# How a two-phase spectral kernel loads its input: batch-wise loads, contiguous DFT tables, and two frequency tiles at once

## The chip, the cores and the metric

One core of a Trainium2 chip. The metric is the device time of one execution in microseconds (us), as the median of several executions; the profile is one further execution, seen by the hardware profiler. Where a ratio of two kernels is given, it is the mean time of one kernel's fast runs over that of the other's of the same rounds, so it is not quite the ratio of the medians quoted beside it.

Engines: TensorE multiplies matrices and writes PSUM (its accumulator memory), VectorE and ScalarE do element-wise work, GpSimd and SyncE mainly issue DMAs here. In these kernels the loads issued by GpSimd change the type on the way (f32 in memory, f16 in SBUF, the on-chip memory) and appear in the profile as the software queue (q0); the loads issued by SyncE appear as the hardware queue (q1). The profile gives both as shares of the same 16 DMA engines. A packet is one piece of a transfer, as the profile counts it; when a load has landed is the time of landing that the profile gives for it.

## The reference, cut to what matters

```python
# x: [8, 3008, 256] f32, filt_r, filt_i: [1505, 256]
X = np.fft.rfft(x, axis=1)
y = np.fft.irfft(X * (filt_r + 1j * filt_i), n=3008, axis=1)
h = y.reshape(24064, 256) @ w_in           # [256, 2048]
g = h * sigmoid(beta * h)
out = g @ w_out                            # [2048, 256]
```

## The kernel before

Phase 1 is the forward transform, as a product with cosine and sine tables. There are 12 frequency tiles m of 128 rows, 24 row tiles of x (the last with 64 rows, since 3008 = 23 x 128 + 64), and 8 batches of 256 columns. For each m and each half g of the batches, 96 matmuls of 512 columns sum over the row tiles; VectorE multiplies by the filter, and the results go to memory. Phase 2 (inverse transform and the two products with the weights) follows and is not touched.

```python
for g in range(NCOL_GRP):                        # 2 halves of 4 batches
    for t in range(NT):                          # 24 row tiles
        src = x[b0 : b0 + nb, t * P : t * P + L, :].transpose([1, 0, 2])
        nc.gpsimd.dma_start(out=xt[:L, b0 : b0 + nb, :], in_=src)
# ... weights (GpSimd), beta, inverse tables of the first chunk (2 x 1.5 MB), SyncE ...
for src_ap, dst in ((filt_r, flt_r), (filt_i, flt_i)):
    nc.vector.memset(flt_f32, 0.0)
    for t in range(KT):                          # 12 loads; the last has 97 rows
        L = min(P, NF - t * P)
        nc.sync.dma_start(out=flt_f32[:L, t, :], in_=src_ap[t * P : t * P + L, :])
    nc.vector.tensor_scalar_mul(dst, flt_f32, 1.0 / S)
for m in range(KT):                              # 12 frequency tiles
    nc.sync.dma_start(out=tcs,                   # 256 B pieces
        in_=TC_h.rearrange("(t p) k -> p t k", p=P)[:, :, m * P : (m + 1) * P])
    # ... tss the same way ...
    for g in range(NCOL_GRP):
        for nt in range(NT):
            xt, L = x_tiles[nt]                  # L = 64 for the last
            for chk in range(NCH):               # 2 x 512 columns
                nc.tensor.matmul(psA[:, ocol], lhsT=tcs[:L, nt, :], rhs=rhs, ...)
                nc.tensor.matmul(psB[:, ocol], lhsT=tss[:L, nt, :], rhs=rhs, ...)
        # ... six VectorE operations of 128x1024, two stores ...
```

## Time and profile before

| | us |
|---|---|
| median of 4 runs before the prediction | 1852.07 |
| span of the profiled run | 1846.6 |
| first matmul | 52.3 |
| m=0 done (192 matmuls) | 118.8 |
| one group of 96 matmuls from there | 20.93 |
| last matmul of phase 1 starts | 579.1 |

The prediction shows the lines. A line of the page's slices is a picture in time: a column of PE that is not 9 is where something can be won. Here these are the first three, one at the passage to phase 2, and the last; the change is aimed at the first three. And VectorE's first operation after a group is a good timekeeper for TensorE, because the profile names the group's matmuls as what it waited for, and it starts 0.2 us after the start of the last of them (579.27 after 579.08); the distance between two of them is what a group costs. And the cold clock is this in the trace of the kernel before: from 587.3 to 590.7 us, after waits of 5.8 and 1.5 us, eight matmuls start 0.42 us apart instead of 0.216, at a granted clock of 0.50 (1.00 from 592 to 600), which by these starts costs 1.7 us.

### The profile page before, as it was taken

Reading aid. Unit: us, or ns where it says so; the run is one execution under the profiler, and the core shown is the slowest. Engines: PE = TensorE matmul, PEld = TensorE weight load, DVE = VectorE, ACT = ScalarE, POOL = GpSimd, SP = SyncE. Lnnn points to the kernel's source line nnn. Section 1 sums busy time; section 2 is a strip of 40 time slices with the busy share of each in tenths; the row PEclk is TensorE's granted clock in tenths of the full one; section 3 lists DMA queues with packets and bytes.
Section 4 is the critical chain, followed back from the end, with each engine's and each line's share of the span. In section 5 each row is a group of like instructions: output and inputs, shape, how many; then the busy total and the mean of one; then the engine's idle time right before and its main releaser. Section 6 shows DMA issues by size and latency. Waiting matters only on the chain.

```text
span 1846.6 us, 22328 instructions
## 1 busy us (share of the span) xinstructions
PE 1746.4 (95%) x9216; PEld 846.8 (46%) x9216; DVE 796.1 (43%) x1204; ACT 492.0 (27%) x769; POOL 38.9 (2%) x54
## 2 busy tenths in 40 slices
PE   0789999999998999999999999999999999999997
PEld 0234444444443545454455445544545544554553
DVE  1113333333333454444454455545545544544554
ACT  0000000000000433433343343433334434433443
POOL 3310000000000000000000000000000000000000
PEclk9999999999999999999999999999999999999999
DMA  9992222233204545344633644444462464344420
GB/s 213 203 157 58 63 64 58 57 70 78 70 23 155 153 151 177 121 135 152 192 121 111 194 159 140 149 136 160 151 188 86 150 194 138 115 145 150 160 83 22
DMA packets 314682, 235.49 MB, mean 128 GB/s; under 512 B 82962, under 2 KB 308180, under 8 KB 314580
## 3 DMA queue, kind: packets, MB, share of 16 engines
q1 hardware_dynamic: 287412, 219.65, 40.0%
q0 software_dynamic: 27168, 14.42, 5.7%
q8 instruction: 72, 1.18, 0.3%
q14 instruction: 30, 0.25, 0.0%
HBM read 211.23 MB, written 37.22 MB: 135 GB/s over the span
## 4 chain that ended last, share of the span: by engine, by line
PE 82%; DMA 15%; DVE 2%; issue 1%; ACT 0%; POOL 0%; DVEq 0%; SPq 0%; POOLq 0%
PE pso L305 20%; PE psh L286 15%; PE psA L175 13%; PE psB L182 12%; PE psy L255 11%; PE psy L262 11%; DMA out_dram<-osb 8%; DMA xsb<-in_x_dram 6%; DVE osb L316 1%; DMA Qb<-spec_q 0%; DVE gsb L301 0%; ACT sig L294 0%; POOL xsb L122 0%; DVEq L316 0%; SPq L226 0%
## 5 line engine op out<-in xcount | busy, mean ns | idle before, releaser
L294 ACT ACTIVATE sig<-psh,beta_sb 128x512 f32<-128x512 f32 (+1 forms) x768 | 490.8, 675 | 1229.2 <-PE psh L286 1212.6
L301 DVE TENSOR_TENSOR gsb<-psh,sig 128x512 f16<-128x512 f32 (+1 forms) x768 | 492.6, 675 | 511.8 <-ACT sig L294 481.8
L305 PE MATMUL pso<-wq_sb,gsb 128*128 128x256 f16 (+1 forms) x3072 | 492.0, 275 | 18.9 <-DVE osb L316 14.3
L175 PE MATMUL psA<-xsb,tcs 128*128 128x512 f16 (+1 forms) x1152 | 439.2, 383 | 61.1 <-DMA tcs<-dft_tc 52.3
L286 PE MATMUL psh<-yt,w_in_sb 128*128 128x512 f16 (+1 forms) x1536 | 460.2, 375 | 0.0
L182 PE MATMUL psB<-xsb,tss 128*128 128x512 f16 (+1 forms) x1152 | 437.7, 382 | 6.9 <-DMA tss<-dft_ts 6.9
L262 PE MATMUL psy<-uss,Qb 128*128 128x512 f16 (+1 forms) x1128 | 422.4, 374 | 0.0
L255 PE MATMUL psy<-ucs,Pb 128*128 128x512 f16 (+1 forms) x1128 | 422.3, 374 | 0.0
L305 PEld LDWEIGHTS <-gsb 128*128 128x128 f16 (+1 forms) x3072 | 256.8, 98 | 315.5 <-DVE gsb L301 235.6
L175 PEld LDWEIGHTS <-tcs 128*128 128x128 f16 (+1 forms) x1152 | 113.2, 98 | 205.2 <-DMA tcs<-dft_tc 52.3
L182 PEld LDWEIGHTS <-tss 128*128 128x128 f16 (+1 forms) x1152 | 113.1, 98 | 151.1 <-issue 15.9
L286 PEld LDWEIGHTS <-w_in_sb 128*128 128x128 f16 x1536 | 145.2, 98 | 64.6 <-issue 1.7
L262 PEld LDWEIGHTS <-Qb 128*128 128x128 f16 x1152 | 112.8, 98 | 130.3 <-issue 6.9
L196 DVE TENSOR_TENSOR t<-psA,flt_r 128x1024 f32<-128x1024 f32 x24 | 29.4, 1224 | 330.3 <-PE psA L175 330.3
L255 PEld LDWEIGHTS <-Pb 128*128 128x128 f16 x1152 | 112.8, 98 | 126.9 <-issue 6.6
L316 DVE COPY osb<-pso 128x256 f32<-128x256 f32 x192 | 73.8, 419 | 84.1 <-DMA out_dram<-osb 74.2
L270 DVE CAST yt<-psy 128x512 f16<-128x512 f32 (+1 forms) x96 | 64.6, 673 | 43.2 <-PE psy L262 43.2
L122 POOL DMA_DIRECT2D xsb<-in_x_dram x48 | 36.8, 774 | 69.2 <-DMA xsb<-in_x_dram 68.4
L294 ACT ACT_TABLE_LOAD x1 | 1.3, 1283 | 117.8 <-DMA xsb<-in_x_dram 117.8
L199 DVE TENSOR_TENSOR t<-psA,flt_i 128x1024 f32<-128x1024 f32 x24 | 29.4, 1225 | 0.8
L201 DVE TENSOR_TENSOR qst<-t,qst 128x1024 f16<-128x1024 f32 x24 | 29.4, 1224 | 0.8
L198 DVE TENSOR_TENSOR pst<-pst,t 128x1024 f16<-128x1024 f16 x24 | 29.2, 1216 | 0.0
(13 smaller groups left out, 89.7 us busy)
## 6 DMA issues: line engine op xcount, KB each, us to landing
ucs<-dft_uc SPq DMA_DIRECT2D x39, 1536.0 KB, 6.7
uss<-dft_us SPq DMA_DIRECT2D x39, 1536.0 KB, 9.7
out_dram<-osb SPq DMA_DIRECT2D x184, 128.0 KB, 4.5
xsb<-in_x_dram POOLq DMA_DIRECT2D x46, 256.0 KB, 18.3
ucs<-dft_uc SPq DMA_DIRECT2D x8, 1344.0 KB, 6.3
uss<-dft_us SPq DMA_DIRECT2D x8, 1344.0 KB, 8.2
tcs<-dft_tc SPq DMA_DIRECT2D x12, 768.0 KB, 6.7
tss<-dft_ts SPq DMA_DIRECT2D x12, 768.0 KB, 9.6
```

The source lines that it names most:

```text
L122: nc.gpsimd.dma_start(out=xt[:L, b0 : b0 + nb, :], in_=src)
L175: nc.tensor.matmul(psA[:, ocol], lhsT=tcs[:L, nt, :], rhs=rhs, start=(nt == 0), stop=(nt == NT - 1),)
L182: nc.tensor.matmul(psB[:, ocol], lhsT=tss[:L, nt, :], rhs=rhs, start=(nt == 0), stop=(nt == NT - 1),)
L196: nc.vector.tensor_tensor(t1, Av, frb, op=mybir.AluOpType.mult)
L255: nc.tensor.matmul(psy[:, :nl], lhsT=Pb[:, kt, dh * P : (dh + 1) * P], rhs=ucs[:, kt, :nl], start=(kt == 0), stop=False,)
L262: nc.tensor.matmul(psy[:, :nl], lhsT=Qb[:, kt, dh * P : (dh + 1) * P], rhs=uss[:, kt, :nl], start=False, stop=(kt == KT - 1),)
L270: nc.vector.tensor_copy(yt[:, :nl], psy[:, :nl])
L286: nc.tensor.matmul(psh[:, :nl], lhsT=w_in_sb[:, dh, t * P : (t + 1) * P], rhs=yT[dh][:, :nl], start=(dh == 0), stop=(dh == NDH - 1),)
L294: nc.scalar.activation(out=sig[:, :nl], in_=psh[:, :nl], func=mybir.ActivationFunctionType.Sigmoid, scale=beta_sb[:, t : t + 1],)
L301: nc.vector.tensor_mul(gsb[:, :nl], psh[:, :nl], sig[:, :nl])
L305: nc.tensor.matmul(pso[u][:mu, :], lhsT=gsb[:, m0 : m0 + mu], rhs=wq_sb[:, t, :], start=(t == 0), stop=(t == NFT - 1),)
L316: nc.vector.tensor_copy(osb[:mu], pso[u][:mu, :])
```

## The change

Its intent is to feed TensorE earlier. (1) x is loaded batch by batch, in one load of 23 row tiles each; the last 64 rows of all batches come first, into a tile whose other 64 rows are zeros, so that all matmuls have 128 rows. (2) The forward tables are laid out so that each partition reads one piece of 6144 B. (3) The filters are loaded by the software queue, type change included, behind batch 1. (4) beta and the inverse tables move to m=4. (5) A group has two batches, and the groups of m=0 and m=1 are done together, so that each pair of batches feeds both as it arrives.

```diff
+    def col_blocks(T):
+        T = T.reshape(NT, P, KT, P).transpose(2, 1, 0, 3)
+        return np.ascontiguousarray(T.reshape(KT * P, NT * P))
...
-        for g in range(NCOL_GRP):
-            for t in range(NT):
-                src = x[b0 : b0 + nb, t * P : t * P + L, :].transpose([1, 0, 2])
-                nc.gpsimd.dma_start(out=xt[:L, b0 : b0 + nb, :], in_=src)
+        nc.vector.memset(x_sb[LREM:, NTF, :, :], 0.0)
+        nc.gpsimd.dma_start(out=x_sb[:LREM, NTF, :, :], in_=x[:, NTF * P :, :].transpose([1, 0, 2]))
+        for b in range(B):
+            if b == 2:
+                # per filter: memset, one load of 11 tiles, one of 97 rows (both gpsimd), scaling
+            nc.gpsimd.dma_start(out=x_sb[:, :NTF, b, :],
+                in_=x[b, : NTF * P, :].rearrange("(t p) d -> p t d", p=P))
...
-                in_=TC_h.rearrange("(t p) k -> p t k", p=P)[:, :, m * P : (m + 1) * P],
+                in_=TC_h[m * P : (m + 1) * P, :].rearrange("p (t k) -> p t k", k=P),
...
+        for g in range(NG):                      # 4 pairs of batches
+            for j in range(n_pair):              # m = 0 and 1
+                fwd_group(j, g, *pair_cols[j], jtag=str(j))
+        for m in range(n_pair, KT):
+            tcs, tss = load_cols(m)
+            for g in range(NG):
+                stored = fwd_group(m, g, tcs, tss, jtag="0")
+                if m == 4 and g == 0:
+                    with tc.issue_after(...):    # beta and the inverse tables
```

More of the change, by code (lines that the diff above doesn't have):

```diff
@@ L69 @@
     NT = (S + P - 1) // P
+    NTF = S // P
+    LREM = S - NTF * P
     KT = (NF + P - 1) // P
@@ L75 @@
     TCn, TSn, UCn, USn = _dft_tables(S, NF)
+    def col_blocks(T):
+        T = T.reshape(NT, P, KT, P).transpose(2, 1, 0, 3)
+        return np.ascontiguousarray(T.reshape(KT * P, NT * P))
+    TCn, TSn = col_blocks(TCn), col_blocks(TSn)
     TC_h = nc.inline_tensor(TCn, name="dft_tc").ap()
@@ L90 @@
     MMN = 512
-    NCOL_GRP = 2 if (B % 2 == 0 and BD // 2 >= MMN) else 1
-    nb = B // NCOL_GRP
-    GW = nb * D
-    bpc = max(1, min(nb, MMN // D))
-    assert nb % bpc == 0
-    NCH = nb // bpc
+    bpc = max(1, min(B, MMN // D))
+    assert B % bpc == 0
+    NG = B // bpc
+    GWID = bpc * D
     n_chunks = (S + MMN - 1) // MMN
@@ L104 @@
         xsb_pool = ph1.enter_context(tc.tile_pool(name="xsb", bufs=1))
-        col_pool = ph1.enter_context(tc.tile_pool(name="cols", bufs=2))
+        colA_pool = ph1.enter_context(tc.tile_pool(name="colsA", bufs=2))
+        colB_pool = ph1.enter_context(tc.tile_pool(name="colsB", bufs=1))
         flt_pool = ph1.enter_context(tc.tile_pool(name="flt", bufs=1))
@@ L108 @@
         tmpf_pool = ph1.enter_context(tc.tile_pool(name="tmpf", bufs=2))
-        psA_pool = ph1.enter_context(tc.tile_pool(name="psA", bufs=2, space=bass.MemoryType.PSUM))
-        psB_pool = ph1.enter_context(tc.tile_pool(name="psB", bufs=2, space=bass.MemoryType.PSUM))
-        x_tiles = []
-        for t in range(NT):
-            L = min(P, S - t * P)
-            xt = xsb_pool.tile([P, B, D], DT, name=f"xsb{t}")
-            x_tiles.append((xt, L))
-        for g in range(NCOL_GRP):
-            b0 = g * nb
-            for t in range(NT):
-                xt, L = x_tiles[t]
-                src = x[b0 : b0 + nb, t * P : t * P + L, :].transpose([1, 0, 2])
-                nc.gpsimd.dma_start(out=xt[:L, b0 : b0 + nb, :], in_=src)
+        psF_pool = ph1.enter_context(tc.tile_pool(name="psF", bufs=2, space=bass.MemoryType.PSUM))
+        x_sb = xsb_pool.tile([P, NT, B, D], DT, name="x_sb")
+        nc.vector.memset(x_sb[LREM:, NTF, :, :], 0.0)
+        if LREM > 0:
+            nc.gpsimd.dma_start(
+                out=x_sb[:LREM, NTF, :, :],
+                in_=x[:, NTF * P :, :].transpose([1, 0, 2]),
+            )
+        for b in range(B):
+            if b == 2:
+                flt_r = flt_pool.tile([P, KT, D], DT, name="flt_r")
+                flt_i = flt_pool.tile([P, KT, D], DT, name="flt_i")
+                KTF = NF // P
+                for src_ap, dst in ((filt_r, flt_r), (filt_i, flt_i)):
+                    nc.vector.memset(dst, 0.0)
+                    if KTF > 0:
+                        nc.gpsimd.dma_start(
+                            out=dst[:, :KTF, :],
+                            in_=src_ap[: KTF * P, :].rearrange("(t p) d -> p t d", p=P),
+                        )
+                    if NF > KTF * P:
+                        LL = NF - KTF * P
+                        nc.gpsimd.dma_start(out=dst[:LL, KTF, :], in_=src_ap[KTF * P :, :])
+                    nc.vector.tensor_scalar_mul(dst, dst, 1.0 / S)
+            if NTF > 0:
+                nc.gpsimd.dma_start(
+                    out=x_sb[:, :NTF, b, :],
+                    in_=x[b, : NTF * P, :].rearrange("(t p) d -> p t d", p=P),
+                )
         w_in_sb = wsb_pool.tile([P, NDH, DFF], DT, name="w_in_sb")
@@ L128, with load_cols @@
         beta_sb = wsb_pool.tile([P, NFT], F32, name="beta_sb")
-        nc.sync.dma_start(out=beta_sb, in_=moe_beta.rearrange("(t p) -> p t", p=P))
+        def load_cols(m, pool=colA_pool, tag_suffix="0"):
+            tcs = pool.tile([P, NT, P], DT, name=f"tcs{tag_suffix}", tag=f"tcs{tag_suffix}")
+            tss = pool.tile([P, NT, P], DT, name=f"tss{tag_suffix}", tag=f"tss{tag_suffix}")
+            nc.sync.dma_start(
+                out=tcs,
+                in_=TC_h[m * P : (m + 1) * P, :].rearrange("p (t k) -> p t k", k=P),
+            )
+            nc.sync.dma_start(
+                out=tss,
+                in_=TS_h[m * P : (m + 1) * P, :].rearrange("p (t k) -> p t k", k=P),
+            )
+            return tcs, tss
+        pair_cols = (
+            [load_cols(0), load_cols(1, colB_pool, "1")] if KT > 1 else [load_cols(0)]
+        )
         pre_uc = pre_pool.tile([P, KT, MMN], DT, name="pre_uc")
@@ L133 @@
         nl0 = min(MMN, S)
-        nc.sync.dma_start(
-            out=pre_uc[:, :, :nl0],
-            in_=UC_h.rearrange("(t p) n -> p t n", p=P)[:, :, 0:nl0],
-        )
-        nc.sync.dma_start(
-            out=pre_us[:, :, :nl0],
-            in_=US_h.rearrange("(t p) n -> p t n", p=P)[:, :, 0:nl0],
-        )
-        flt_f32 = flt_pool.tile([P, KT, D], F32, name="flt_f32", tag="flt_tmp")
-        flt_r = flt_pool.tile([P, KT, D], DT, name="flt_r")
-        flt_i = flt_pool.tile([P, KT, D], DT, name="flt_i")
@@ L146, with fwd_group @@
-        for src_ap, dst in ((filt_r, flt_r), (filt_i, flt_i)):
-            nc.vector.memset(flt_f32, 0.0)
-            for t in range(KT):
-                L = min(P, NF - t * P)
-                nc.sync.dma_start(out=flt_f32[:L, t, :], in_=src_ap[t * P : t * P + L, :])
-            nc.vector.tensor_scalar_mul(dst, flt_f32, 1.0 / S)
-        for m in range(KT):
-            tcs = col_pool.tile([P, NT, P], DT, name="tcs", tag="tcs")
-            tss = col_pool.tile([P, NT, P], DT, name="tss", tag="tss")
+        def fwd_group(m, g, tcs, tss, jtag):
+            psA = psF_pool.tile([P, MMN], F32, name=f"psA{jtag}", tag=f"psA{jtag}")
+            psB = psF_pool.tile([P, MMN], F32, name=f"psB{jtag}", tag=f"psB{jtag}")
+            b0 = g * bpc
+            for nt in range(NT):
+                L = P
+                rhs = x_sb[:L, nt, b0 : b0 + bpc, :]
+                nc.tensor.matmul(
+                    psA[:, :GWID],
+                    lhsT=tcs[:L, nt, :],
+                    rhs=rhs,
+                    start=(nt == 0),
+                    stop=(nt == NT - 1),
+                )
+                nc.tensor.matmul(
+                    psB[:, :GWID],
+                    lhsT=tss[:L, nt, :],
+                    rhs=rhs,
+                    start=(nt == 0),
+                    stop=(nt == NT - 1),
+                )
+            Av = psA[:, :GWID].rearrange("p (b d) -> p b d", b=bpc)
+            Bv = psB[:, :GWID].rearrange("p (b d) -> p b d", b=bpc)
+            frb = flt_r[:, m, :][:, None, :].to_broadcast([P, bpc, D])
+            fib = flt_i[:, m, :][:, None, :].to_broadcast([P, bpc, D])
+            pst = stg_pool.tile([P, bpc, D], DT, name="pst", tag="pst")
+            qst = stg_pool.tile([P, bpc, D], DT, name="qst", tag="qst")
+            t1 = tmpf_pool.tile([P, bpc, D], F32, name="t1", tag="t1")
+            nc.vector.tensor_tensor(t1, Av, frb, op=mybir.AluOpType.mult)
+            nc.vector.tensor_tensor(pst, Bv, fib, op=mybir.AluOpType.mult)
+            nc.vector.tensor_add(pst, pst, t1)
+            nc.vector.tensor_tensor(t1, Av, fib, op=mybir.AluOpType.mult)
+            nc.vector.tensor_tensor(qst, Bv, frb, op=mybir.AluOpType.mult)
+            nc.vector.tensor_sub(qst, t1, qst)
+            colsl = slice(b0 * D, (b0 + bpc) * D)
@@ L156 @@
             nc.sync.dma_start(
-                out=tcs,
-                in_=TC_h.rearrange("(t p) k -> p t k", p=P)[:, :, m * P : (m + 1) * P],
-            )
-            nc.sync.dma_start(
-                out=tss,
-                in_=TS_h.rearrange("(t p) k -> p t k", p=P)[:, :, m * P : (m + 1) * P],
-            )
-            for g in range(NCOL_GRP):
-                psA = psA_pool.tile([P, GW], F32, name="psA", tag="psA")
-                psB = psB_pool.tile([P, GW], F32, name="psB", tag="psB")
-                b0 = g * nb
-                for nt in range(NT):
-                    xt, L = x_tiles[nt]
-                    for chk in range(NCH):
-                        cb = chk * bpc
-                        rhs = xt[:L, b0 + cb : b0 + cb + bpc, :]
-                        ocol = slice(chk * bpc * D, (chk + 1) * bpc * D)
-                        nc.tensor.matmul(
-                            psA[:, ocol],
-                            lhsT=tcs[:L, nt, :],
-                            rhs=rhs,
-                            start=(nt == 0),
-                            stop=(nt == NT - 1),
-                        )
-                        nc.tensor.matmul(
-                            psB[:, ocol],
-                            lhsT=tss[:L, nt, :],
-                            rhs=rhs,
-                            start=(nt == 0),
-                            stop=(nt == NT - 1),
-                        )
-                Av = psA[:].rearrange("p (b d) -> p b d", b=nb)
-                Bv = psB[:].rearrange("p (b d) -> p b d", b=nb)
-                frb = flt_r[:, m, :][:, None, :].to_broadcast([P, nb, D])
-                fib = flt_i[:, m, :][:, None, :].to_broadcast([P, nb, D])
-                pst = stg_pool.tile([P, nb, D], DT, name="pst", tag="pst")
-                qst = stg_pool.tile([P, nb, D], DT, name="qst", tag="qst")
-                t1 = tmpf_pool.tile([P, nb, D], F32, name="t1", tag="t1")
-                nc.vector.tensor_tensor(t1, Av, frb, op=mybir.AluOpType.mult)
-                nc.vector.tensor_tensor(pst, Bv, fib, op=mybir.AluOpType.mult)
-                nc.vector.tensor_add(pst, pst, t1)
-                nc.vector.tensor_tensor(t1, Av, fib, op=mybir.AluOpType.mult)
-                nc.vector.tensor_tensor(qst, Bv, frb, op=mybir.AluOpType.mult)
-                nc.vector.tensor_sub(qst, t1, qst)
-                colsl = slice(b0 * D, (b0 + nb) * D)
-                nc.sync.dma_start(
-                    out=P_h[m * P : (m + 1) * P, colsl],
-                    in_=pst[:].rearrange("p b d -> p (b d)"),
-                )
-                nc.sync.dma_start(
-                    out=Q_h[m * P : (m + 1) * P, colsl],
-                    in_=qst[:].rearrange("p b d -> p (b d)"),
-                )
@@ new lines, in fwd_group @@
+                out=P_h[m * P : (m + 1) * P, colsl],
+                in_=pst[:].rearrange("p b d -> p (b d)"),
+            )
+            return nc.sync.dma_start(
+                out=Q_h[m * P : (m + 1) * P, colsl],
+                in_=qst[:].rearrange("p b d -> p (b d)"),
+            )
+        n_pair = len(pair_cols)
+        for g in range(NG):
+            for j in range(n_pair):
+                tcs, tss = pair_cols[j]
+                fwd_group(j, g, tcs, tss, jtag=str(j))
+        for m in range(n_pair, KT):
[3 more added lines that the diff above has]
+                if m == 4 and g == 0:
+                    with tc.issue_after(stored.ins if hasattr(stored, "ins") else stored):
+                        nc.sync.dma_start(out=beta_sb, in_=moe_beta.rearrange("(t p) -> p t", p=P))
+                        for pre, U_h in ((pre_uc, UC_h), (pre_us, US_h)):
+                            nc.sync.dma_start(
+                                out=pre[:, :, :nl0],
+                                in_=U_h.rearrange("(t p) n -> p t n", p=P)[:, :, 0:nl0],
+                            )
```

## The prediction

> **What bounds the kernel now.** I read the page's slices and chain first, then TensorE's waits in the opening, then the opening's DMA counts.
>
> The page, busy tenths in 40 slices of 46 us, and the chain:
>
> ```profile
> PE   0789999999998999999999999999999999999997
> ...
> DMA  9992222233204545344633644444462464344420
> PE 82%; DMA 15%; DVE 2%; issue 1%; ACT 0%; POOL 0%; DVEq 0%; SPq 0%; POOLq 0%
> PE pso L305 20%; PE psh L286 15%; PE psA L175 13%; PE psB L182 12%; PE psy L255 11%; PE psy L262 11%; DMA out_dram<-osb 8%; DMA xsb<-in_x_dram 6%; DVE osb L316 1%; DMA Qb<-spec_q 0%; DVE gsb L301 0%; ACT sig L294 0%; POOL xsb L122 0%; DVEq L316 0%; SPq L226 0%
> ```
>
> TensorE bounds everything except the first three slices, where it starves and the DMA engines are full; the 6% of x loads on the chain are those slices. The change touches only phase 1 (forward DFT), so I look at its start. The waits up to 118.8 us:
>
> ```profile
> PE psA L175 <- DMA tcs<-dft_tc: 52.3, 1, 52.3
> ...
> PE psA L175 <- DMA xsb<-in_x_dram: 8.6, 11, 1.3
> ...
> PE psB L182 <- DMA tss<-dft_ts: 6.9, 1, 6.9
> ```
>
> TensorE starts at 52.3 (first cosine columns), stops again until 65.0 (sine columns), then trickles behind x. VectorE's timeline gives the end of each group (a group is 96 matmuls: one frequency tile m, four batches):
>
> ```profile
> 118.82 1.22 DVE L196 TENSOR_TENSOR t<-psA,flt_r 128x1024 f32<-128x1024 f32 x1 [26.80 <-PE psA L175]
> ...
> 139.75 1.22 DVE L196 TENSOR_TENSOR t<-psA,flt_r 128x1024 f32<-128x1024 f32 x1 [13.79 <-PE psA L175]
> ...
> 579.27 1.23 DVE L196 TENSOR_TENSOR t<-psA,flt_r 128x1024 f32<-128x1024 f32 x1 [13.79 <-PE psA L175]
> ```
>
> m=0 is done at 118.8; from there 22 groups take 460.45 us, 20.93 each, with no hole. Two groups of work (41.9 us) took 118.8: the opening loses 77 us, and that is all there is to win in phase 1.
>
> What makes x late? Software-queue packets (x, 512 B written each) in three windows, 10 to 25, 72 to 76 and 95 to 103 us; columns are packets, MB, share of 16 engines:
>
> ```profile
> q0 software_dynamic: 2608, 1.30, 62.5%
> q1 hardware_dynamic: 2609, 2.58, 62.3%
> ...
> q0 software_dynamic: 1516, 0.75, 139.2%
> q1 hardware_dynamic: 63, 0.05, 4.9%
> ...
> q0 software_dynamic: 2153, 1.07, 108.1%
> q1 hardware_dynamic: 156, 0.10, 5.3%
> ```
>
> Nearly alone, x moves 1516/4 = 379 packets per us; in 116 to 119 it is 1111/3 = 370, or 43.2 ns per packet on each of 16 engines. Beside 1 KB hardware packets it gets 174, one for one. In 95 to 103 it gets only 269, although the hardware queue has 20 packets per us. My reading: those are the leftovers of one engine, and a load of x ends when its slowest engine ends. GpSimd's issues in this stretch, each waiting for an older x load, come every 2.15 us (94.47, 96.58, 98.77, 100.91): one load has 512/16 = 32 packets per engine, so the slow engine does 15 per us where 23 are possible. The filter's last rows are 97 partitions, twelve small loads per filter.
>
> [...] the profile does not name engines, so it is an inference. [...] after 8 us idle at 579 us matmuls start 0.43 us apart instead of 0.216. [...] x's last 64 rows are 64-row matmuls, and steps into and out of them are 0.31 us:
>
> ```profile
> 558.15 0.38 PE L182 MATMUL psB<-xsb,tss 64*128 64x512 f16 x1
> 558.46 0.39 PE L175 MATMUL psA<-xsb,tcs 128*128 128x512 f16 x1
> 558.68 0.38 PE L182 MATMUL psB<-xsb,tss 128*128 128x512 f16 x1
> ```
>
> **The change part by part.**
> 1. Matmuls: 12 tiles x 4 groups x 48 = 2304 of 512 columns, as before. The padded tail makes all of them 128-row. Two steps of +0.095 us per 96 matmuls go: a group of 48 costs 48 x 0.216 = 10.36 us instead of 10.47. Over m=2..11 (40 groups) 414.5 us instead of 418.6: 4 us saved on the path, nearly sure.
> 2. Column tables: 6144 B contiguous per partition instead of 24 pieces of 256 B. Four loads (m=0,1), probably six (m=2 has a free buffer): 768 packets, 48 per engine; at the 1 KB packet's 42 ns, 24.4 GB/s, one takes 252 ns: 12.1 us per engine in all, done near 17 us when alternating with x. The 52.3 and 65.0 us waits go.
> 3. The 3 MB of preloaded inverse tables leaves the opening (3072 packets x 42 ns / 16 = 8 us), and lands in m=4, where DMA is at 26%. Filters: twelve hardware loads each become software loads behind batch 1: 3010 packets, 8.1 us of the software queue.
> 4. x by whole batch, groups of two batches, m=0 and 1 together: each arriving pair of batches feeds 96 matmuls, 20.7 us, instead of a trickle for one m.
> 5. VectorE: six operations of 1.22 us become twelve of some 0.65 per 20.7 us: hidden. PSUM still has two buffers per tag.
> 6. The passage to phase 2 (579.3 to 587.3, waiting for Qb) stays: Pb and Qb still take space of the x tiles and wait for the last matmul.
>
> Arrivals, per engine: x tail 32 packets, each batch 184, filters 188. Batches 0,1: 3 (first packet) + 400 x 43.2 ns = 17.3 + 12.1 (tables) + 2 (landing) = 34. Batches 2,3: 956 packets, 41.3, + 12.1 + 1.3 (stores) + 3 + 2 = 60, and up to 64 if each 97-row filter load again sits on one engine (91 extra packets, 4 us). Batches 4,5: 76 to 80. Batches 6,7: 93 to 98.
> TensorE: group 0 from 34, +20.7 +2.3 (cold clock) = 57; group 1 waits for batches 2,3, 60 to 64, then is continuous: + 3 x 20.7 + 0 to 2 (cold again) = 122 to 128. Batches 4 to 7 come in time. Then 414.5: phase 1 ends at 537 to 543 instead of 579.3. Sum: 36 to 43 us, centre 40, so 1852 - 40 = 1812.
>
> **The rivals.**
> A. x stays the bound at its present pace: if the lag is not one engine but the engines' rate with casting (213 packets per us over 24,064 in 113 us), the last batches land near 115, and phase 1 ends at 115 + 20.7 + 414.5 = 550: gain 29, 1823. For: the share is above 90% throughout. Against: 370 in two windows.
> B. The one x tile is tracked as a whole, or by the span of its strided slices, and the first matmul waits for all of x: start 97, end 97 + 83 + 414.5 = 594, 1867. Against: at 579.48 Pb's strided load of batch 0 is issued before the stores of batches 4 to 7 into the same rows at 583.92, so strided pieces are told apart.
> C. The columns of m=2 are issued in order behind the last stores of the pair: TensorE would stall some 10 us after the pair, 1822. Against: the columns of m=1 went out at 68.88 us, before the stores of m=0 at 89.53.
> D. TensorE fills the hole before batches 2,3 with m=2's first group, if the static order allows: no hole at all, phase 1 ends near 34 + 2.3 + 48 x 10.36 = 534: gain 45, 1807. For: the order is not the program's in the kernel before (13 psA, then 13 psB); against: that needs the hole foreseen.
>
> **Range and chances.** 2% is 1815.0, and the sum gives 1809 to 1816 with nothing else going wrong: slightly more than even. A or C in part give 1822 or so, D 1807. Prediction 1812, range 1803 to 1825; faster 0.54, within 2% 0.45, slower 0.01 (B).
>
> **What would show it.** First matmul near 34 us; the wait before group 1 small, 3 to 7 us, and by x; the last batch landed before 100; software packets above 300 per us from 20 us on; no 64-row matmul and 10.36 us from group to group; columns of m=2 landed before 25 us; the Qb wait still about 8 us. I am wrong if group 1 starts after 70, if TensorE waits again after the pair, or if phase 2 (579.3 to the end, 1267 us) changes by more than 3 us.

## The result, and the profile after

The changed kernel takes 1804.52 us (median of 8 runs, 1803.5 to 1806.71) where the kernel before takes 1851.27 (12 runs): ratio 0.975, 95% interval 0.974 to 0.976. That is faster by over 2%, and within the predicted range, near its low end: 46.7 us won where 40 were predicted.

The page's slices and chain after:

```profile
PE   2999999999989999999999999999999999999997
...
DMA  9941321111127356336434643643454354443420
...
PE 85%; DMA 12%; DVE 2%; issue 1%; ACT 0%; DVEq 0%; SPq 0%; POOLq 0%
```

From the second slice on PE is at 9, but for the passage to phase 2 and the last slice. The DMA engines are full for two slices instead of three. TensorE's only wait in the first 125 us, and the two places where it falls (timeline of TensorE; the bracket is the idle time and what ended it):

```profile
PE psA L181 <- DMA x_sb<-in_x_dram: 32.6, 2, 31.7
```

```profile
31.71 0.59 PE L181 MATMUL psA<-x_sb,tcs 128*128 128x512 f16 x1 [31.71 <-DMA x_sb<-in_x_dram]
...
56.22 0.38 PE L181 MATMUL psA<-x_sb,tcs 128*128 128x512 f16 x1 [0.94 <-DMA x_sb<-in_x_dram]
```

The tables no longer appear: TensorE waits for batches 0 and 1 until 31.7, and batches 2 and 3 come 0.94 us late. From there nothing is missing. The ends of groups on VectorE:

```profile
118.36 0.69 DVE L202 TENSOR_TENSOR t<-psA,flt_r 128x512 f32<-128x512 f32 x1 [6.42 <-PE psA L181]
...
128.72 0.69 DVE L202 TENSOR_TENSOR t<-psA,flt_r 128x512 f32<-128x512 f32 x1 [6.42 <-PE psA L181]
...
532.76 0.69 DVE L202 TENSOR_TENSOR t<-psA,flt_r 128x512 f32<-128x512 f32 x1 [6.42 <-PE psA L181]
```

At 118.4 us both m=0 and m=1 are done, where before m=0 alone was done at 118.8: one m more, 2 x 20.93 = 41.9 us of work. After it 40 groups take 414.4 us, 10.36 each, where 40 half groups took 418.6: 4.2 us. Together 46.1, which is the whole shift of the end of phase 1 (last matmul at 532.6 instead of 579.1) but 0.4.

The software queue from 24 to 48 us, while batches and filters pass:

```profile
q0 software_dynamic: 9402, 4.75, 145.5%
```

That is 9402/24 = 392 packets per us, 41 ns per packet and engine, with nothing beside it.

### The profile page after: what moved, and what is told of

Read it like the earlier page. It is cut to its first block, busy times and chain, and to the rows that moved or that the text cites.

```text
span 1804.9 us, 22521 instructions
## 1 busy us (share of the span) xinstructions
PE 1737.0 (96%) x9216; PEld 850.4 (47%) x9216; DVE 809.3 (45%) x1349; ACT 492.8 (27%) x769; POOL 18.4 (1%) x19
## 4 chain that ended last, share of the span: by engine, by line
PE 85%; DMA 12%; DVE 2%; issue 1%; ACT 0%; DVEq 0%; SPq 0%; POOLq 0%
PE pso L330 21%; PE psh L311 16%; PE psA L181 13%; PE psB L188 13%; PE psy L280 11%; PE psy L287 11%; DMA out_dram<-osb 9%; DMA x_sb<-in_x_dram 3%; DVE osb L341 1%; DMA Qb<-spec_q 0%; DVE gsb L326 0%; ACT sig L319 0%; DVEq L341 0%; SPq L251 0%; DVEq L326 0%
## 5 line engine op out<-in xcount | busy, mean ns | idle before, releaser
L181 PE MATMUL psA<-x_sb,tcs 128*128 128x512 f16 x1152 | 438.3, 380 | 32.6 <-DMA x_sb<-in_x_dram 32.6
L188 PE MATMUL psB<-x_sb,tss 128*128 128x512 f16 x1152 | 438.1, 380 | 0.0
L181 PEld LDWEIGHTS <-tcs 128*128 128x128 f16 x1152 | 113.0, 98 | 168.6 <-issue 33.6
L188 PEld LDWEIGHTS <-tss 128*128 128x128 f16 x1152 | 113.0, 98 | 137.9 <-issue 2.9
L202 DVE TENSOR_TENSOR t<-psA,flt_r 128x512 f32<-128x512 f32 x48 | 33.2, 692 | 307.6 <-PE psA L181 307.6
L205 DVE TENSOR_TENSOR t<-psA,flt_i 128x512 f32<-128x512 f32 x48 | 33.2, 691 | 1.7
L207 DVE TENSOR_TENSOR qst<-t,qst 128x512 f16<-128x512 f32 x48 | 33.2, 691 | 1.6
L204 DVE TENSOR_TENSOR pst<-pst,t 128x512 f16<-128x512 f16 x48 | 32.7, 682 | 0.0
L206 DVE TENSOR_TENSOR qst<-psB,flt_r 128x512 f16<-128x512 f32 x48 | 32.7, 681 | 0.0
```

The source lines that it names most:

```text
L181: nc.tensor.matmul(psA[:, :GWID], lhsT=tcs[:L, nt, :], rhs=rhs, start=(nt == 0), stop=(nt == NT - 1),)
L188: nc.tensor.matmul(psB[:, :GWID], lhsT=tss[:L, nt, :], rhs=rhs, start=(nt == 0), stop=(nt == NT - 1),)
L202: nc.vector.tensor_tensor(t1, Av, frb, op=mybir.AluOpType.mult)
L205: nc.vector.tensor_tensor(t1, Av, fib, op=mybir.AluOpType.mult)
```

## The experiments

Eleven runs were made (one of them the changed kernel again), all with correct results. For each I give the median and the ratio to the kernel before of the same rounds, and where the last matmul of phase 1 starts in its trace ("end of phase 1": 579.1 before, 532.6 after). Phase 2 is the same code in all of them.

### One engine's lag (b_split97)

```diff
-                nc.sync.dma_start(out=flt_f32[:L, t, :], in_=src_ap[t * P : t * P + L, :])
+                L16 = L - L % 16
+                nc.sync.dma_start(out=flt_f32[:L16, t, :], in_=src_ap[t * P : t * P + L16, :])
+                if L > L16:
+                    nc.sync.dma_start(out=flt_f32[L16:L, t, :], in_=src_ap[t * P + L16 : t * P + L, :])
```

> The kernel before, with nothing changed but the last filter load of each filter: 97 rows as 96 rows and 1 row[...]. My theory (one engine lags with the 97-row loads and what queues behind them, and every load of x ends with it): x then costs each engine 1504 packets x 41 ns = 62 us, and the hardware packets of that time 31 us (pre-tables 8, filters 8, the tables of m=0 and 1 15), so the last batches land near 98 instead of 117, m=0 ends near 102 instead of 118.8, and the whole is 12 to 18 us faster: 1833 to 1839. Rival A (the engines themselves move casting packets at the pace seen, 213 per us on average): nothing changes, within 2 us of before. Between: 3 to 10 us if the 97 rows are only one of several causes of lag.

Measured: 1840.60 against 1848.46, 7.9 us faster, ratio 0.9957 (0.9943 to 0.9971); end of phase 1 570.9, 8.2 earlier. The direction is that of the theory; the size is not, and lies in the band (3 to 10 us) that I had set for one of several causes. The trace shows the reasons for both. First its windows 68 to 84 and 96 to 104 us:

```profile
q0 software_dynamic: 3886, 1.93, 87.4%
q1 hardware_dynamic: 3885, 0.99, 46.5%
...
q0 software_dynamic: 3155, 1.57, 145.0%
```

When the tables are through, x runs alone at 3155/8 = 394 per us, with no hardware packet left; in the kernel before the prediction saw 269 in the same stretch, with a trickle of 20 hardware packets per us beside it. Nothing but two loads of 97 rows had been split, so a lag of x comes from these loads. That it is one engine that lags is read from the packet lists of the kept traces, which do not name engines: in the kernel before, the 256 B packets between 95 and 103 us start one at a time, 67 ns apart, about the 66 ns that a pair of packets, one of x and one of a table, takes on an engine (below), and from 32 to 38 us the last 1 KB packets of the first filter pass the same way, 95 ns apart; in b_split97 the tables still pass at 244 packets per us from 84 to 88 us, and from 96 us there are none.

Why one engine holds up all of x is in the times of the loads: in the kernel before, from the tenth load on, almost every load of GpSimd is issued 0.3 us after the load eight before it has landed (for example landed at 94.18, next one issued at 94.47). So eight loads, 8 x 32 packets per engine, are in flight, and when one engine is that far behind, the others run out of x: at 109.5 us x falls to 30 packets per us, with 4 hardware packets per us beside it.

The size: while tables pass, the two queues move packet for packet, 3886/16 = 243 pairs per us, so a pair takes 16/243 = 66 ns on an engine, and a 256 B table packet adds 66 - 41 = 25 ns to a packet of x. In the window 10 to 25 us of the kernel before, 174 pairs per us give 92 ns, so a 1 KB packet adds 51. (The single engine's packets, 67 and 95 ns apart, give 26 and 54.) I had reckoned 20 and 42: 20 was an estimate, and 42 is what a 1 KB packet takes nearly alone (in the kernel before 370 of them and 10 of x per us from 5.8 to 6.8 us, 16/380 = 42 ns). With the measured costs I estimate that an engine needs 62 + 380 x 51 ns (inverse tables and filters) + 768 x 25 ns = 100 us for what passes until x is in, not 93. The last load of x landed at 109.4 (117.7 before): the lag was worth 8 us, and most of the rest of the wait was packets.

### The tables alone (b_tab)

The edit is the change's part 2 in the kernel before: `col_blocks` and the two `in_=` lines of the diff above.

> The kernel before, with the forward tables alone laid out so that each partition reads 6144 B in one piece. My theory: the tables of m=0 and 1 are 32 packets per engine instead of 768, which frees 9 us of every engine, and above all leaves the engine with the 97-row loads far fewer packets to alternate with x, so x is throttled much less: the last batches land near 100, first matmul before 45 us, 12 to 20 us faster in all (1831 to 1839). Rival (only the bytes and the first wait count, the lag is elsewhere or is not one engine): the first matmul comes earlier, but m=0 still ends with x near 110 or later: at most 6 to 8 us faster.

Measured: 1837.31, 11.1 us faster, ratio 0.9938 (0.9924 to 0.9952); end of phase 1 567.8. That is 1 us short of my range and above the rival's 6 to 8; but the last load of x landed at 106.4 and m=0 was done at 107.6, nearer to the rival's 110 than to my 100. First matmul at 42.4 as expected, but the lag does not vanish. Its windows 64 to 76 and 88 to 96:

```profile
q0 software_dynamic: 2746, 1.36, 95.5%
q1 hardware_dynamic: 40, 0.08, 2.0%
...
q0 software_dynamic: 3153, 1.57, 144.9%
q1 hardware_dynamic: 7, 0.00, 0.2%
```

From 64 to 76 x gets only 229 per us, and later 394. The 40 hardware packets of the first window again start one at a time, the last at 69.2 us. After it x has the engines to itself and still falls to 26 per us at 70.5 to 71.5 us, about the pace of one engine (1000/41 = 24): the lagging engine is working off its part of the loads in flight. Splitting the 97 rows won 8.2 us of phase 1 and laying out the tables 11.3. Both leave the lagging engine less to do, so they may overlap; no run has both in the kernel before.

### The inverse tables early (a_pre)

In the changed kernel, beta and the inverse tables are loaded ahead of the forward tables:

```diff
+        nc.sync.dma_start(out=beta_sb, in_=moe_beta.rearrange("(t p) -> p t", p=P))
+        for pre, U_h in ((pre_uc, UC_h), (pre_us, US_h)):
+            nc.sync.dma_start(out=pre[:, :, :nl0],
+                in_=U_h.rearrange("(t p) n -> p t n", p=P)[:, :, 0:nl0])
         def load_cols(m, pool=colA_pool, tag_suffix="0"):
...
-                if m == 4 and g == 0:
-                    with tc.issue_after(...):    # the same loads
```

> The changed kernel with the inverse tables for the first chunk (3 MB) and beta loaded at the start, ahead of the forward tables, as in the kernel before. My theory (3072 packets of 1 KB take 8 us of every engine and delay all that comes after): batches 0,1 land near 40 instead of 31.7, batches 2,3 near 64, then TensorE runs without holes: 8 to 9 us slower than the changed kernel, near 1813. Rival (the engines had room[...]): under 3 us.

Measured: 1814.28 against 1848.52, ratio 0.9813 (0.9796 to 0.9829); end of phase 1 544.4, 11.8 later than in the changed kernel. First matmul at 43.1, 11.4 later. The theory holds; most of the size is again that of the 1 KB packet at 51 ns: 192 per engine x 51 = 9.8 us instead of 8. The other 1.6 us were not tested apart; beta, which this edit moves too, goes first as 2048 packets of 4 B and lands at 3.9 us.

### The filters in the hardware queue (a_fltHW)

```diff
-                    nc.vector.memset(dst, 0.0)
-                    nc.gpsimd.dma_start(out=dst[:, :KTF, :], ...)
-                    nc.gpsimd.dma_start(out=dst[:LL, KTF, :], ...)
-                    nc.vector.tensor_scalar_mul(dst, dst, 1.0 / S)
+                    nc.vector.memset(flt_f32, 0.0)
+                    for t in range(KT):
+                        L = min(P, NF - t * P)
+                        nc.sync.dma_start(out=flt_f32[:L, t, :], in_=src_ap[t * P : t * P + L, :])
+                    nc.vector.tensor_scalar_mul(dst, flt_f32, 1.0 / S)
```

> The changed kernel with the filters loaded as in the kernel before: 12 hardware-queue loads each into an f32 tile, the last of 97 rows. If one engine's lag by the 97-row loads were enough by itself, x would be throttled from about 20 us on and batches 2,3 would land 5 to 10 us later, 5 to 10 us slower in all. My theory says that the lag grows only while the lagging engine has many other hardware packets to alternate with (the tables are now 48 packets per engine and land first): batches 2,3 land within 4 us of the changed kernel's 55.6, and the whole is within 5 us of it, 1802 to 1809.

Measured: 1812.60 against 1848.52, ratio 0.9805 (0.9791 to 0.9820); end of phase 1 543.9, 11.3 later. I was wrong: batch 3 landed at 66.4, 10.2 us later than in the changed kernel, and the whole is more than 5 us slower, so the numbers of the other side are the nearer ones. But TensorE does not wait for batches 2 and 3, where I looked. It has one wait, at the start:

```profile
PE psA L177 <- DMA x_sb<-in_x_dram: 45.4, 1, 45.4
```

In the software queue the filters stand behind batch 1. In the hardware queue they stand in no line with x at all: their 1 KB packets pass beside batches 0 and 1 (from 9 to 18 and from 36 to 45 us) and delay them to 45.4. The lag is there too. From 29 to 36 us:

```profile
q0 software_dynamic: 2621, 1.33, 139.9%
q1 hardware_dynamic: 21, 0.11, 4.0%
```

Of the 21 packets 18 are 6144 B pieces of tables (0.11 MB; the others are 4 B). In the packet list they start one at a time, 0.28 us apart, the last at 34.1 us. That is the pace of one engine: in the changed kernel's trace 16 engines, alternating with x from 6 to 14 us, did 55 per us, or 3.4 each. So one engine has a backlog, while x as a whole runs at 2621/7 = 374 per us and not at 269 as in the kernel before. A load of x is now 184 packets per engine instead of 32, so that the loads in flight keep the other engines busy; that this makes the difference was not tested. How much of the 11.3 is the lag and how much the filters' place in front was not separated.

### Without the pair (a_nopair)

```diff
-        pair_cols = (
-            [load_cols(0), load_cols(1, colB_pool, "1")] if KT > 1 else [load_cols(0)]
-        )
+        pair_cols = [load_cols(0)]
```

> The changed kernel without the pairing: m=0 alone first, m=1 after it like the others. My theory (each arriving pair of batches must feed 96 matmuls or TensorE starves): x lands as before, the last pair near 89 us, m=0 ends there + 10.4 = near 100 instead of 118.4 for m=0 and 1 together; the remaining 44 groups x 10.36 us = 456: phase 1 ends near 556 instead of 532.6, 21 to 25 us slower than the changed kernel, 1826 to 1830. Rival (the pairing only reorders work, the gain came from the transfers alone): within 5 us of the changed kernel.

Measured: 1820.96 against 1848.52, ratio 0.9849 (0.9834 to 0.9864); end of phase 1 551.4, 18.8 later than with the pair. Three fifths of the gain survive without the pair, two fifths need it. TensorE's restarts:

```profile
27.97 0.58 PE L179 MATMUL psA<-x_sb,tcs 128*128 128x512 f16 x1 [27.97 <-DMA x_sb<-in_x_dram]
51.52 0.58 PE L179 MATMUL psA<-x_sb,tcs 128*128 128x512 f16 x1 [10.93 <-DMA x_sb<-in_x_dram]
67.94 0.58 PE L179 MATMUL psA<-x_sb,tcs 128*128 128x512 f16 x1 [3.62 <-DMA x_sb<-in_x_dram]
84.01 0.59 PE L179 MATMUL psA<-x_sb,tcs 128*128 128x512 f16 x1 [2.96 <-DMA x_sb<-in_x_dram]
```

From the second on, pairs of batches arrive 16 us apart and feed 10.4 us of work each. After a hole the matmuls are also slower at first: from 51.52 to 56.17 eleven of them start 0.42 us apart, and then 0.22, and the group that began at 67.94 ended at 80.9, 12.9 us instead of 10.4. Of the expected 21 to 25 us, 18.8 came, because x itself is in 5 us earlier (last load landed at 83.9 instead of 89.1): two tables fewer stand before it.

### The 64-row matmuls, from both sides (b_pad, a_tail64)

In the kernel before (b_pad):

```diff
             xt = xsb_pool.tile([P, B, D], DT, name=f"xsb{t}")
+            if L < P:
+                nc.vector.memset(xt[L:, :, :], 0.0)
...
-                        rhs = xt[:L, b0 + cb : b0 + cb + bpc, :]
+                        rhs = xt[:, b0 + cb : b0 + cb + bpc, :]
...
-                            lhsT=tcs[:L, nt, :],
+                            lhsT=tcs[:, nt, :],
```

In the changed kernel (a_tail64):

```diff
-                L = P
+                L = P if nt < NTF else LREM
```

> The kernel before, with the last 64 rows of x padded by zeros to 128 rows in SBUF, so that all matmuls of phase 1 have 128 rows. My theory (each step into and out of the 64-row form costs 0.095 us on TensorE): 22 to 24 groups x 0.19 us = 4.2 to 4.6 us faster, 1846.7 to 1847.1 where before is 1851.3; groups 20.73 us apart instead of 20.93. Rival (the steps hide behind something else, such as the reads at a group's end): no change.

> The changed kernel, with the last tile of x used as 64 rows again (the zero rows are there but not read). My theory (two steps of 0.095 us per group, and the groups are now 48 matmuls): 48 groups x 0.19 us = 9 us slower, 1813.6 where the changed kernel is 1804.5; groups 10.55 us apart instead of 10.36. Rival (the cost goes by the number of 64-row matmuls, which is the same as before): 4.5 us slower. Second rival: no change.

Measured: b_pad 1843.46 against 1848.46, 5.0 us faster, ratio 0.9972 (0.9958 to 0.9986), end of phase 1 574.8 (4.3 earlier), groups 20.72 us apart. a_tail64 1812.08 against the same 1848.46, ratio 0.9801 (0.9788 to 0.9814), where the changed kernel has 0.975; end of phase 1 541.7, 9.1 later. Groups in a_tail64 are 10.57 us apart (108.6, 119.2, 129.7). Its steps:

```profile
107.88 0.38 PE L188 MATMUL psB<-x_sb,tss 128*128 128x512 f16 x1
108.19 0.39 PE L181 MATMUL psA<-x_sb,tcs 64*128 64x512 f16 x1
108.41 0.38 PE L188 MATMUL psB<-x_sb,tss 64*128 64x512 f16 x1
108.72 0.39 PE L181 MATMUL psA<-x_sb,tcs 128*128 128x512 f16 x1
```

Starts are 0.31 us apart at each change of form and 0.22 within one. The number of 64-row matmuls is the same 96 in the kernel before and in a_tail64; the number of changes is doubled, and so is the cost. It goes by the change, not by the matmul.

### The changed kernel again, and m=2's tables later (after_again, a_m2late)

```diff
-                fwd_group(j, g, tcs, tss, jtag=str(j))
+                last = fwd_group(j, g, tcs, tss, jtag=str(j))
+            if g == 1:
+                with tc.issue_after(...last...):
+                    cols2 = load_cols(n_pair)
```

> The changed kernel itself, once more, beside the others of this group: ratio 0.975 to before again (0.973 to 0.977), and its phase 2 as long as that of the kernel before within 2 us, if the 5.5 us by which phase 2 was longer in the first profile of the changed kernel are chance. If they belong to the change, phase 2 is again near 1260 us from its first matmul to its last, against 1255.

> The changed kernel with the columns of m=2 issued behind the last store of the second pair's first two groups, not at the start. My theory (a 6144 B packet costs each engine some 220 ns wherever it stands; 16 packets fewer at the start): first matmul at 28.0 as in the run without pairing, which also had 16 packets fewer, batches 2,3 near 52, the pair done near 114.7 and no wait for m=2's columns: 3 to 4 us faster than the changed kernel. Rival (the early columns ride along for free): the same within 1 us. Rival C of the prediction (late columns stall TensorE after the pair): slower.

Measured: after_again 1804.58 against 1849.95, ratio 0.9755 (0.9742 to 0.9768), phase 1 the same to 0.1 us. Its phase 2, from first matmul to last, is 1258.8 us, after 1260.6 in the first profile and 1255.0 in the kernel before; the other variants of the changed kernel, with the same phase 2, have 1252.2 to 1258.2, those of the kernel before 1254.2 to 1257.1. So neither expectation was met cleanly: there is a scatter of some us from run to run. The medians of all runs say more than single profiles: the whole gain is 46.7 us in the first comparison and 45.4 here, where phase 1 gives 46.5, so that about 1 us at most is left for a longer phase 2. a_m2late: first matmul at 28.0, end of phase 1 528.2, 4.4 earlier; 1802.18, 2.4 faster by the medians, ratio 0.9741 (0.9727 to 0.9754). The trace says that the early tables do not ride for free, and that late ones stall nothing; the intervals of the two ratios overlap, so in the whole time the gain is likely but not shown.

### A version that streams (a_stream, a_stream2)

The wait left is the first 31.7 us. Two batches must be in before anything starts, although one row tile of them is enough for four matmuls.

```diff
+        PIECES = [(0, 6), (6, 12), (12, 18), (18, 23)]   # a_stream2: (0, 2), (2, 6), ...
+        for g in range(NG):
+            for k, (ta, tb) in enumerate(PIECES):
+                for b in range(g * bpc, (g + 1) * bpc):
+                    nc.gpsimd.dma_start(out=x_sb[:, ta:tb, b, :],
+                        in_=x[b, ta * P : tb * P, :].rearrange("(t p) d -> p t d", p=P))
+            # behind g == 1: the filters; the pair's tables in the same pieces
...
+            for nt in range(NT):
+                for j in range(n_pair):                  # m = 0 and 1, tile by tile
+                    # matmul into psA of j, matmul into psB of j
```

> A version that goes further: every pair of batches in four pieces of x's row tiles, the pair's tables in matching pieces, the matmuls of m=0 and 1 taken tile by tile, the filters behind the second pair, the columns of m=2 after the second pair. If TensorE can eat x as it lands (a row tile of two batches is 256 packets, 0.66 us at 389 per us, and feeds four matmuls, 0.86 us), the first matmul comes near 12 us instead of 31.7, the four pairs end near 100 instead of 118.4: 14 to 18 us faster than the changed kernel, 1787 to 1791. If the pieces cost more than they bring (tables of 1.5 KB pieces, cold clock through small holes, filters late for the third pair's PSUM), 5 us or less.

> The streaming version with the first piece of every pair cut down to two row tiles, tables likewise: the first matmul at 9 to 11 us instead of 16.0, so up to 5 us faster than the streaming version (1783.6 beside 1848.5, ratio 0.9653): ratio 0.9625 to 0.9645. If TensorE only starts earlier and then waits for x in many small holes at the cold clock, the ratio stays at 0.965.

Measured: a_stream 1783.60 against 1848.52, ratio 0.9653 (0.9635 to 0.9670), end of phase 1 517.4, 15.1 earlier than the changed kernel, within the 14 to 18 expected. The first matmul is at 16.0, not 12, the fourth pair is done at 103.0, and one of the feared costs came: the filters land at 54.5 us, after the first pair is done (38.6), so VectorE starts late, and at 62.2 us TensorE waits 2.1 us for it to free PSUM. Four edits are in this version; the late tables of m=2 alone gave 4.4 us (a_m2late), and the rest was not separated. The smaller loads cost x no pace: from 24 to 32 us, with loads of 384 KB written, several of them in flight, the software queue moved 3144/8 = 393 packets per us, as with 1472 KB in the changed kernel (392). This version is the fastest kernel together with a_stream2: 1785.02 against 1849.95, ratio 0.9650 (0.9637 to 0.9663), end of phase 1 516.7. The smaller first piece was a miss. TensorE's waits in the first 62 us of a_stream2:

```profile
7.42 0.58 PE L195 MATMUL psA<-x_sb,tcs 128*128 128x512 f16 x1 [7.42 <-DMA x_sb<-in_x_dram]
...
12.96 0.59 PE L195 MATMUL psA<-x_sb,tcs 128*128 128x512 f16 x1 [1.97 <-DMA x_sb<-in_x_dram]
...
23.11 0.58 PE L195 MATMUL psA<-x_sb,tcs 128*128 128x512 f16 x1 [4.92 <-DMA x_sb<-in_x_dram]
```

It starts 8.6 us sooner, and then waits twice more, because x and tables share the engines until 21 us; each restart begins with a matmul of 0.58 us. The rival of the expectation holds.

## Why the prediction was right

By its own steps:

- **What makes x late.** That one engine lags, and by the loads of 97 rows, was a guess from the pace of x; b_split97 bears it out. But the lag is 8 of the 77 us that the opening lost; the larger part was packets in front of x and beside it.
- **Part 1, the padding.** Predicted 4 us, measured 4.2 in the groups, and confirmed from both sides. (So the 77 us of the opening were not "all there is to win in phase 1", as the prediction says before it comes to this part.)
- **Part 2, the tables.** The waits at 52.3 and 65.0 went, m=2's tables went out at the start (issued at 3.3 and 3.8 us), and all had landed by 16.7 us. Predicted near 17. The packet cost was right (6144 B: 16/55 = 291 ns for a packet with its share of x, less 1.09 packets of x at 41, since 481 of x went with 442 of these, = 246; I said 252), but x's first packet came at 5.6, not at 3, so that the first tables had the engines to themselves.
- **Part 3, tables and filters moved.** Right in kind. a_pre and a_fltHW show that each is worth over 11 us in the changed kernel (the tables together with beta); the inverse tables were put at 8. The term that was too small is the 1 KB hardware packet beside x, 51 ns instead of 42. It did not enter the sum, since these loads no longer stand in front.
- **Part 4, the pair.** Right: with it x's arrival (89.1 us) no longer bounds, and TensorE is continuous from 56.2.
- **Parts 5 and 6.** VectorE's operations are 0.69 us and hidden. The passage to phase 2 stays: TensorE waits 5.1 us for Pb and 1.5 more for Qb. Before it was 5.8 and 1.5, but the 5.8 ended with VectorE's last read of psA (585.15); Pb had landed at 584.4. The prediction puts the whole passage down to Qb.
- **The sum.** Batches 0 and 1 came at 31.7 instead of 34, batches 2 and 3 at 56.2 instead of 60 to 64, and the pair was done at 118.4 instead of 122 to 128. This is where nearly all of the 7.5 us between 1812 and 1804.5 lie (0.8 are the kernel before, 1851.3 instead of 1852.1). Two terms were too large: a packet of x takes 41.1 ns alone, not 43.2 (956 x 2.1 ns = 2 us), and the allowance of up to 4 us for 97-row loads on one engine did not come: x ran at 392 per us right through them, and each landed 0.2 us after the filter load before it. The 3 us for the first packet are its time in the kernel before (2.96); the 2 us for landing were an allowance that rested on no trace named there. The slow matmuls at the start cost 2.7 us (13 of them from 31.71 to 37.20, 5.5 us instead of 2.8), where 2.3 were put. With batches 2 and 3 only 0.94 us late there was no second slow start either (0 to 2 us were allowed): from 56.22 on the matmuls start 0.22 us apart at once.

Of the rivals, A was the one to be taken seriously, and b_split97 disposes of it: the engines can move x at 394 per us in the kernel before. B, C and D did not occur; a_m2late shows that C's stall does not come even with the tables late. D's number (534 us, 1807) is nearer to the result than the prediction's own, but by chance: the hole before batches 2 and 3 was short because they came early, and nothing of m=2 was done in it. The prediction calls itself wrong if phase 2 changes by more than 3 us; in the profiled runs it did (5.6 and 3.8 us longer), which has no explanation, while the medians leave about 1 us.

Two parts were never taken out of the changed kernel: the contiguous tables and the loading by batches. And not all of the gain can be shared out. Taken alone in the kernel before, tables and split 97 rows win 11.3 and 8.2 us of phase 1; taken out of the changed kernel, the pair costs 18.8, the filters 11.3, the inverse tables 11.8, the padding 9.1. The last four make 51.0, more than the 46.5 that all parts win together. For the padding the reason is shown (9.1 here and 4.3 in the kernel before, by the number of groups); for the others it was not tested.

## What to carry to other kernels

When TensorE starves at the start as here, count packets per engine and not bytes alone (here, beside a packet of x, 25 ns for one of 256 B, 51 for 1 KB, 246 for 6144 B): which queue, how large, and what stands in front of the first data needed. Look for loads whose row count differs from the others', and split them to see. Here two loads of 97 rows on the hardware queue held up the loads of x on the other queue: split into 96 rows and 1, they made phase 1 8.2 us shorter (b_split97). On the software queue loads of 97 rows cost nothing that could be seen (x at 392 packets per us while they passed, in the changed kernel). Then give each piece that arrives as much work as the transfer of the next piece takes, and make the first piece small; below what the tables beside it allow, smaller won nothing (a_stream2).
